# Zero rows, first loads and chunk loads of a kernel that joins delta-rule attention, a routed expert layer and a gated layer

## The chip, the cores and the metric

One core of a Trainium2 chip runs the whole program. The metric is the time of one execution on the device in microseconds (us); the median of three runs is quoted. The engines are TensorE (PE, matmuls; PEld its weight loads), VectorE (DVE), ScalarE (ACT), GpSimd (POOL) and SyncE (SP), which only issues transfers here.

## The reference, cut to what matters

Attention (4 batches, 8 heads, 768 steps, 48 wide) is a recurrence over a 48 x 48 state:

```
for t in range(S):
    y[t]  = q[t] @ state
    state = state + beta[t] * outer(k[t], v[t] - k[t] @ state)      # k normalised
```

Its 3072 x 384 output goes through eight experts, each token through the one with the largest gate logit:

```
h  = relu(x[mask] @ w1[e]);  ye = h @ w2[e]                # 384 -> 1024 -> 384
out[mask] = gate_w[mask] * sigmoid(x @ w_output_gate)[mask, e] * ye
```

and the result through `(sigmoid(x @ w_gate) * (x @ w_val)) @ w_out` with 1536 hidden columns.

## The kernel before

**Attention** runs over `NCH` = 12 chunks of 64 steps, all heads and batches at once. For a chunk c: PE adds what the old state gives to the negated values (`KU`), ACT copies that to `W`, PE applies the upper half of the inverse of a triangular matrix (`XT`, `XW`), ACT copies the result to `UF`, PE couples the two 32-step halves (`GS`), and `W`, `XT` and `UF` come once more; then PE updates the state sum (`Sps`), ACT copies it to `SH`, and PE makes the chunk's output rows (`GY`), which ACT copies to `XG`. So a chunk is one chain that goes to and fro between PE and ACT. Beside it run: the Gram products of chunk c + `LA` = c + 5 on PE (`GY<-KQ`), copied to `G`, `GS` and `PM`; on DVE the inverse for each pair of chunks, about 31 column steps of two instructions (`X<-X,tmp`, `tmp<-X,Lt`), one part of it on POOL (`tmpG`); the masks `PM`; the scaling of the values `VT`; and the gates of the expert layer. All engines' orders in attention are fixed at build time by a list with due times (`Filler`); a helper on line 78 records each operation, so most rows bear L78.

**Loads in attention** are issued by SP, in the program's order: for each chunk K and Q (`KQ`, four transfers of 192 KB into a ring of `RK` = 7 buffers), `VT` and `kt` (eight transfers of 48 KB each, two buffers each). `load_kq(c + 6)` stands in the first half of chunk c, `load_v(c + 2)` and `load_k(c + 2)` at its end. The state's products read all 128 partitions of a `KQ` buffer, so the 16 partitions without data must be zero: POOL clears buffers 2 to 6 at the start, and `load_pad` loads zeros into buffers 0 and 1.

**Rows for the experts** go to `disp` in DRAM: expert e has a region of 3584 rows, and each token is scattered (by POOL) to the next free row of its expert. An expert is then read as one window of fixed length (up to 512 rows), so the rows behind its last token must hold zeros. `zero_fill` writes 512 rows of zeros (772 KB) at the start of each of the eight regions, before any token is scattered: two at the end of chunks 0, 1 and 2, two at the start of chunk 3.

**Experts** (`Experts.run`) run over nine jobs: expert 0 in two parts of 256 and 208 rows, then seven experts in the order of their counts with windows of 460 to 380 rows. `rows` loads a job's window from `disp` to `XR`; `load` loads a quarter of an expert's weights (`w1r`, `w2r`, 384 KB each, two buffers each), which ACT and DVE or POOL split in a high and a low part. SP issues these, and takes the expert's number and the row from `tab` by a register load. The last stage (L1333, L1362) is matmuls without a gap worth naming.

Of the kernel before, what the change touches and what calls it, by code (L numbers as in the profile page):

```python
# [22 lines left out]
NE, DF = 8, 1024  # L23
# [108 lines left out]
class Attention:  # L132
# [5 lines left out]
    def run(self, small, acc, zero_fill, small_loads):  # L138
# [39 lines left out]
        quads = [(2 * a + k, 2 * y + r) for a in range(4) for r in range(2) for k, y in ((0, 0), (1, 1), (0, 1), (1, 0))]  # L178
        pairs = [(4 * z + j, z ^ y) for j in range(4) for z in range(2) for y in range(2)]

        def load_kq(c, k=slice(0, 2)):
            for r in range(2):
                d = slice(64 * r, 64 * r + 48)
                for i in range(2):
                    SP.dma_start(
                        out=KQ[c % RK][d, k].rearrange("d k p (i t) h -> d k p i (t h)", i=2)[:, :, :, i],
                        in_=a["st"][2 * c + i, d].rearrange("d (k p x) -> d k p x", k=2, p=2)[:, k])

# [11 lines left out]
                for i in range(2):  # L200
                    SP.dma_start(out=t[quad(at(b), i), par(b)], in_=a[name][32 * b : 32 * b + 32, 2 * c + i])

        def load_k(c):
            KTOK[c] = wk.tile([128, 2, 384], F32, tag="kt", name="kt", bufs=2)
            load_tok(KTOK[c], "ktok", c, pos)

        def load_v(c):
            VT[c] = wk.tile([128, 2, 384], F32, tag="VT", name="VT", bufs=2)
            load_tok(VT[c], "vtok", c, pos)

        def k_turn(c):
# [336 lines left out]
                f()  # L548

        busy(two("KU")[:, 0], W0)  # L550
        for i in range(2, RK):
            G.memset(KQ[i].rearrange("p k y t h -> p (k y t h)"), 0.0)
        for e in range(2):
            load_kq(e, slice(0, 1))
        for x in range(2):
            for i in range(2):
                for r in range(2):
                    for c2 in range(2):
                        d, o = 64 * x + 32 * i + 16 * c2 + 8 * r, 32 * (2 * x + r) + 8 * (2 * c2 + i)
                        SP.dma_start(out=be[d : d + 8], in_=a["beta"][o : o + 8])  # L560
        for t in SHT:
            V.memset(t.rearrange("p y h e -> p (y h e)"), 0.0)
        SHz = SHT[0].rearrange("p y h e -> p y (h e)")
# [1 line left out]
        zrow = ep.tile([128, 2 * ROW], F32, name="zrow")  # L565
        G.memset(zrow, 0.0)
        small_loads(V, SP)
        for e in range(2):
            load_kq(e, slice(1, 2))
        load_kq(2)  # L570
        load_v(0)
        load_kq(3)
        load_kq(4)
        load_k(0)
        load_kq(5)
# [59 lines left out]
            A.copy(out=W, in_=KU[:, :, 0:384])  # L635
            return W.rearrange("p k (a r e) -> p k a r e", a=4, r=2)

        load_pad(1)
        KU = kv(0)
        Wv = w_evac(KU)  # L640
        k_turn(0)
# [12 lines left out]
        for c in range(NCH):  # L654
# [3 lines left out]
            if c == NCH - 2:  # L658
                early.close()

            for e in (6, 7) if c == 3 else ():
                zero_fill(SP, e, zrow)
            beside(c, "load", engines)
            S0 = SH
            if c > 0:
# [21 lines left out]
                Yp = two("GY")  # L687
                y_mm(pairs[:8])
            beside(c, "KS", engines)
            if c > 0 and c + RK - 1 < NCH:  # L690
                load_kq(c + RK - 1)
            for h, b in sorted(quads, key=lambda x: x[0] % 2) if c == 0 else quads:
                mm(out=at(KUv, quad(pos(b), 0), h, b), lhsT=xt(c, h, b, 0), rhs=at(Wv, quad(cross(h, b), 0), h, b), start=True, stop=True)
            if c == 0:
# [4 lines left out]
            A.copy(out=UF, in_=KU[:, :, 0:384])  # L699
            if more:  # L700
                gp_evac(c + LA, 0, P)
            if not last:
                vm = fil.add([(0.9, 0.0, lambda c=c: v_mul(c + 1, (0, 1), V))])
            if c > 0:
# [27 lines left out]
            beside(c, "U", engines)  # L732
            if more:
                gp_evac(c + LA, 1, P)
            if c > 0:
                gate_l(2 * c - 2, mm)
                if c % 2 == 1 and 1 < c < NCH - 3:
                    gate_r(g - 1, mm)
                gate_t(2 * c - 1)
# [15 lines left out]
            if more or c == 0:  # L755
                Yp = two("GY")
                if c > 0:
                    y_mm()
                    A.copy(out=seen, in_=Yp[:, :, 383:384])
            if c > 0:  # L760
                gate_l(2 * c - 1, mm)
# [12 lines left out]
            if last:  # L774
# [5 lines left out]
                scatter(2 * c - 2)  # L780
                scatter(2 * c - 1)
                break
            if c == 1:
                load_pad(0)
            if c + 2 < NCH:
                load_v(c + 2)
                load_k(c + 2)
            if c == 0:
                zero2, other2, ops2 = inv_ops(2, SHE[2])
                fil.add(sum(prep(2), []) + [later(ops2)], WP0)  # L790
                zero2()
            elif (c + LA) % 2 == 1 and (c + LA) // 2 < NG:
                e = (c + LA) // 2
                zero, other, inv = inv_ops(e, SHE[e])
                zero()
                fil.add(sum(prep(e), []) + [later(inv)], WP)
            for e in range(2 * c, min(2 * c + 2, 6)):
                zero_fill(SP, e, zrow)
            beside(c, "end", engines)
            beside(c, "W", engines) if not last else None  # L800
            if more:
# [88 lines left out]
class Experts:  # L890


    def __init__(self, tc, a, disp, perm, idt, sp, jobs):
        self.tc, self.a, self.disp, self.perm, self.idt, self.sp, self.jobs = tc, a, disp, perm, idt, sp, jobs
        self.ahead = min(2, len(jobs))
        nc = tc.nc
        self.use((nc.vector, nc.scalar, nc.gpsimd, nc.tensor, nc.sync))
        self.blocks = [(k, j) for k in range(len(jobs)) for j in range(4) if not jobs[k].shares]
        self.raw, self.W, self.XR, self.X = {}, {}, {}, {}
        self.n_raw = self.n_split = self.nw = 0  # L900
        self.keep = {}

    def use(self, engines):
        self.V, self.A, self.G, self.T, self.SP = engines

    def rows(self, k):
        job = self.jobs[k]
        XR = self.sp.tile([XMAX // 4, 4, ROW], F32, tag="XR", name="XR", bufs=self.ahead)[0 : job.read // 4]
        self.SP.dma_start(out=XR.rearrange("p r c -> p (r c)"), in_=self.disp[ds(job.row, job.read)].rearrange("(p r) c -> p (r c)", r=4))
        self.XR[k] = XR  # L910
        self.X[k] = [self.sp.tile([128, 3, WMAX], F32R, tag=t, name=t, bufs=self.ahead)[:, :, 0 : job.n] for t in ("xh", "xl")]

    def x_scale(self, k, engines):
        n = self.jobs[k].n // 4
# [23 lines left out]
        for c in range(3):  # L938
            self.x_turn(k, c)

    def load(self, upto):

        sp = self.sp
        while self.n_raw < min(upto, len(self.blocks)):
            k, j = self.blocks[self.n_raw]
            r1 = sp.tile([128, 3, 256], F32, tag="w1r", name="w1r", bufs=2)
            r2 = sp.tile([128, 2, 384], F32, tag="w2r", name="w2r", bufs=2)
            one = lambda w: w[ds(self.jobs[k].e, 1)].rearrange("o a b -> (o a) b")
            self.SP.dma_start(out=r1, in_=one(self.a["w1"])[:, 256 * j : 256 * j + 256].rearrange("(c p) f -> p c f", p=128))
            self.SP.dma_start(out=r2, in_=one(self.a["w2"])[256 * j : 256 * j + 256].rearrange("(k p) d -> p k d", p=128))  # L950
            self.raw[self.n_raw] = r1, r2
            self.n_raw += 1
# [95 lines left out]
def kernel_body(tc, a, out):  # L1048
    nc = tc.nc
    V, A, G, T, SP = nc.vector, nc.scalar, nc.gpsimd, nc.tensor, nc.sync  # L1050
    with ExitStack() as ctx:
# [11 lines left out]
        if True:  # L1063
# [17 lines left out]
            def beside(c, at, engines, ps=None):  # L1081

                V, A, G, T, SP = engines
                at = c - NCH, at
                if at == (-2, "load"):
                    sp = moe.enter_context(tc.tile_pool(name="ex_s", bufs=1, side="left", reuse_waits="tile"))
                    ex.append(Experts(tc, a, disp, perm, small["idt"], sp, jobs))
                    ex[0].use(engines)
                    ex[0].load(2)
                elif at == (-2, "U"):  # L1090
                    ex[0].high(0)
                elif at == (-2, "W"):
                    ex[0].low(0, 0, V)
                    ex[0].low(0, 1, V)
                elif at == (-2, "rows"):
                    ex[0].load(3)
                    ex[0].rows(0)
                elif at == (-2, "end"):
                    ex[0].high(1)
                elif at == (-1, "KS"):  # L1100
                    ex[0].x_scale(0, (V,))
                elif at == (-1, "U"):
                    ex[0].low(1, 0, V)
                    ex[0].low(1, 1, V)
                elif at == (-1, "rows"):
                    ex[0].load(4)
                elif at == (-1, "W"):
                    ex[0].x_turn(0, 0, ps)
                elif at == (-1, "V"):
                    ex[0].x_turn(0, 1, ps)  # L1110
                elif at == (-1, "Y"):
                    ex[0].x_turn(0, 2, ps)
# [10 lines left out]
            oh = yp.tile([1, 7, 7], F32, name="oh")  # L1123
            cw = yp.tile([1, 2, 24], F32, name="cw")
            tab = yp.tile([1, 18], I32, name="tab")
            wins, nums, names = [cst[0:1, 296 + 7 * i : 303 + 7 * i] for i in range(3)]

            def order():
# [17 lines left out]
                V.tensor_tensor(out=c[:, 1:2], in0=cnt[:, 0:1], in1=c[:, 0:1], op=ALU.subtract)  # L1146
                V.tensor_scalar_min(out=c[:, 1:2], in0=c[:, 1:2], scalar1=float(E1))
                V.reduce_sum(out=c[:, 2:9], in_=gt, axis=AXX)
                V.tensor_tensor(out=c[:, 2:9], in0=c[:, 2:9], in1=wins, op=ALU.min)
                for i, d in enumerate((1, 2, 4, 8)):  # L1150
                    V.tensor_tensor(out=cw[:, 1 - i % 2, 8:17], in0=cw[:, i % 2, 8:17], in1=cw[:, i % 2, 8 - d : 17 - d], op=ALU.add)
# [4 lines left out]
                    jobs[r + 2].e, jobs[r + 2].row = e, e * STRIDE  # L1156
                for k in range(1, 9):
                    jobs[k].off = nc.values_load(tab[0:1, 7 + k : 8 + k], engines=engs, min_val=0, max_val=NTOK, skip_runtime_bounds_check_because=why)

            def gv_src(i):  # L1160
                b, w = divmod(i, 2)
# [14 lines left out]
            def hook(q, f):  # L1176
# [14 lines left out]
                elif i == 3:  # L1191
                    order()
                    E.rows(1)
                    E.load(6)
                if i == QX:
                    E.x_scale(1, (E.V, E.A))
# [252 lines left out]
```

## Time and profile before

| | |
|---|---|
| median of 3 runs | 985.54 us (985.51 to 987.24) |
| profiled execution: its own time, its span | 988.84 us, 987.1 us |
| PE, DVE, ACT, POOL busy | 932.0, 498.7, 363.5, 386.1 us |
| granted PE clock, mean | 0.933 of full |
| attention | from the start to about 280 us |
| experts, beginning with the end of attention | about 280 to 526 us |
| gated layer | 526 to 977 us |

Busy time says little about PE, since its matmuls overlap. What counts is the time in which an engine waits: a row gives it in brackets with what ended it. The program is one chain of stages, so time that one stage loses, or gains, moves all that follows.

### The profile page before, as it was taken

What the parts mean: (1) busy time and instruction counts of PE and PEld (TensorE: products, weight loads), DVE (VectorE), ACT (ScalarE), POOL (GpSimd) and SP (SyncE); (2) the same over time, 40 slices, a digit from 0 to 9 for tenths busy, and PEclk for the clock granted to TensorE, in tenths of its full rate; (3) what the DMA queues carried; (4) which work ended last, traced back from release to release, by engine and by line L of the source; (5) the groups of instructions that cost most, each with busy time, mean ns of one, the idle gap of its engine ahead of it and who ended that gap; (6) DMA issues with size and microseconds to landing.
All of it is one profiled execution on the core that took longest, in us unless ns stands there. A gap on an engine that the chain in (4) does not pass through costs nothing. (4 is left out here: it accounts for less than half of the span.)

```text
span 987.1 us, 23362 instructions
## 1 busy us (share of the span) xinstructions
PE 932.0 (94%) x9557; PEld 820.6 (83%) x9558; DVE 498.7 (51%) x1387; ACT 363.5 (37%) x670; POOL 386.1 (39%) x550
## 2 busy tenths in 40 slices
PE   6777899988899999999999999999999999999997
PEld 5666687776789899999998888888888888888886
DVE  7999978994354577777865554113113112011112
ACT  2553464554634455555552222112112112111111
POOL 7362364652132455776651434223222212322122
PEclk8697798795879999999999999999999999999999
DMA  5878755224225556466522220000000000000000
GB/s 123 156 168 177 205 119 119 66 71 127 75 90 192 158 167 188 151 202 189 167 66 50 80 64 25 9 1 17 17 1 16 16 1 9 25 1 9 25 1 32
DMA packets 63057, 83.31 MB, mean 84 GB/s; under 512 B 10377, under 2 KB 55698, under 8 KB 62946
## 3 DMA queue, kind: packets, MB, share of 16 engines
q1 hardware_dynamic: 59234, 71.01, 27.2%
q0 software_dynamic: 3712, 10.78, 3.2%
q8 instruction: 75, 1.23, 0.5%
q14 instruction: 36, 0.29, 0.1%
HBM read 64.65 MB, written 15.80 MB: 81 GB/s over the span
## 5 line engine op out<-in xcount | busy, mean ns | idle before, releaser
L1370 DVE TENSOR_TENSOR gf<-gf,g 128x512 f32<-128x512 f32 x72 | 49.4, 686 | 304.9 <-PE g L1362 304.2
L840 POOL TENSOR_TENSOR gsl<-gf,gsh 128x512 fp32r<-128x512 f32 x65 | 84.7, 1304 | 269.7 <-ACT gsh L839 269.7
L1369 ACT ACTIVATE gf<-g 128x512 f32<-128x512 f32 x72 | 43.0, 597 | 181.8 <-PE g L1362 180.4
L839 ACT CAST gsh<-gf 128x512 fp32r<-128x512 f32 x69 | 42.8, 621 | 147.7 <-DVE gf L1370 147.6
L1333 PE MATMUL o<-wol,gsh 128*128 128x384 f32 x272 | 87.1, 339 | 0.0
L1333 PE MATMUL o<-woh,gsl 128*128 128x384 f32 x272 | 86.6, 336 | 0.0
L78 DVE TENSOR_TENSOR X<-X,tmp 128x84 f32<-128x84 f32 (+31 forms) x303 | 72.2, 267 | 0.9
L78 DVE TENSOR_TENSOR tmp<-X,Lt 128x84 f32<-128x84 f32 (+31 forms) x303 | 71.7, 266 | 1.5
L1333 PE MATMUL o<-woh,gsh 128*128 128x384 f32 x272 | 63.3, 340 | 0.0
L969 POOL TENSOR_TENSOR w1l<-w1r,w1h 128x256 fp32r<-128x256 f32 x57 | 52.6, 949 | 25.5 <-ACT w1h L961 21.9
L1362 PE MATMUL g<-yl,wgh 128*128 128x512 f32 x216 | 62.5, 394 | 0.0
L1362 PE MATMUL g<-yl,wvh 128*128 128x512 f32 x216 | 62.4, 395 | 0.0
L1362 PE MATMUL g<-yh,wgh 128*128 128x512 f32 x180 | 60.3, 394 | 0.0
L993 PE MATMUL y<-hh,w2h 128*128 128x460 f32 (+6 forms) x168 | 60.0, 357 | 0.0
L993 PE MATMUL y<-hh,w2l 128*128 128x460 f32 (+6 forms) x168 | 58.5, 348 | 0.0
L1035 DVE SCALAR_TENSOR_TENSOR hl<-h,hh 128x460 fp32r<-128x460 f32 (+7 forms) x57 | 33.0, 579 | 50.0 <-ACT hh L1034 49.9
L78 PE MATMUL GY<-KQ 48*64 48x128 f32 (+1 forms) x640 | 44.3, 405 | 14.5 <-DMA KQ<-in_st_dram 10.8
L1333 PEld LDWEIGHTS o<-woh,gsh 128*128 128x128 f32 x272 | 49.7, 188 | 6.7 <-ACT woh L839 0.6
L1333 PEld LDWEIGHTS o<-wol,gsh 128*128 128x128 f32 x272 | 50.5, 188 | 2.3
L1362 PE MATMUL g<-yh,wgl 128*128 128x512 f32 x180 | 51.8, 394 | 0.0
L1362 PE MATMUL g<-yh,wvl 128*128 128x512 f32 x180 | 51.6, 394 | 0.0
L1362 PE MATMUL g<-yh,wvh 128*128 128x512 f32 x180 | 51.6, 394 | 0.0
(327 smaller groups left out, 2199.0 us busy)
## 6 DMA issues: line engine op xcount, KB each, us to landing
w1r<-in_w_dram SPq DMA_DIRECT2D x32, 384.0 KB
w2r<-in_w_dram SPq DMA_DIRECT2D x32, 384.0 KB
KQ<-in_st_dram SPq DMA_DIRECT2D x40, 192.0 KB
disp<-zrow SPq DMA_DIRECT2D x8, 772.0 KB
VT<-in_vtok_dram SPq DMA_DIRECT2D x96, 48.0 KB
kt<-in_ktok_dram SPq DMA_DIRECT2D x96, 48.0 KB
XG<-in_m2g_dram SPq DMA_DIRECT2D x12, 384.0 KB
XG<-in_m2v_dram SPq DMA_DIRECT2D x12, 384.0 KB
```

What stands on the lines that cost most here:

```text
L78: r = f(*args, **kw)
L839: (act or nc.scalar).copy(out=hi, in_=src)
L840: eng.tensor_tensor(out=lo, in0=src, in1=hi, op=ALU.subtract)
L969: engine.tensor_tensor(out=l[:, k], in0=r[:, k], in1=h[:, k], op=ALU.subtract)
L993: m = self.T.matmul(out=ys[c][:, 0:n], lhsT=w2[l][:, f % 2, 128 * c : 128 * c + 128], rhs=(hh, hl)[r], start=(f == 0 and i == 0), stop=(f ...
L1035: self.behind = self.V.scalar_tensor_tensor(out=hl, in0=hp[:, 0:n], scalar=0.0, in1=hh, op0=ALU.max, op1=ALU.subtract).ins
L1333: T.matmul(out=ops_[m][:, 0:384], lhsT=gh[l][:, 128 * m : 128 * m + 128], rhs=wo[r][:, f], start=(f == 0 and i == 0), stop=(f == 11 and i ...
L1362: T.matmul(out=ps, lhsT=gv[w][l][:, c, 128 * f : 128 * f + 128], rhs=Y[r][c], start=(i == 0 and c == 0), stop=(i == 2 and c == 2))
L1369: A.activation(out=gf, in_=gps[0], func=AF.Sigmoid)
L1370: V.tensor_tensor(out=gf, in0=gf, in1=gps[1], op=ALU.mult)
```

## The change

The rows behind an expert's last token are cleared later and from another source: only expert 0's region is still filled in attention (`zero_fill(SP, 0, zrow)`); for each of the other seven, `clear(k)` copies zeros, once the counts are known, from the padding of the input `st` in DRAM to `disp` from the end of the expert's tokens on, as many rows as the window has. The row where they end comes from a new table `ends` through a register load on SP. `clear(2)` stands behind the load of job 1's rows, each later one behind the load of the job before.

The first loads are split over engines: of the first halves (K) of chunks 0 and 1, SP issues two transfers and ACT two for each; of the 16 transfers of beta ACT issues 4, POOL 4 and SP 8. DVE clears buffer 1 of `KQ`, which did without before, and `load_pad(1)` is gone. The whole loads of `KQ` 2 and 3 move ahead of the second halves (Q) of chunks 0 and 1.

A chunk's loads come in four parts: K of chunk c + 7 behind the state's products of chunk c, `VT` of c + 2 behind the first `UF`, `kt` behind the second, Q of c + 7 behind the products with the state. ACT writes one element of the `VT` or `kt` buffer first (`hold`), and the transfers into that buffer wait for this write. The second quarter of the first expert's weights gets such a hold, too.

```
-        def load_kq(c, k=slice(0, 2)):
+        def load_kq(c, k=slice(0, 2), engines=(SP, SP)):
...
-                    SP.dma_start(
+                    engines[r].dma_start(
...
+        def hold(t):
+
+            A.copy(out=t[0:1, 0, 0:1], in_=idt[0:1, 0:1])
+
-        def load_k(c):
+        def load_k(c, wait=False):
             KTOK[c] = wk.tile([128, 2, 384], F32, tag="kt", name="kt", bufs=2)
+            if wait:
+                hold(KTOK[c])
             load_tok(KTOK[c], "ktok", c, pos)
...
-        for i in range(2, RK):
-            G.memset(KQ[i].rearrange("p k y t h -> p (k y t h)"), 0.0)
+        clear = lambda E, i: E.memset(KQ[i].rearrange("p k y t h -> p (k y t h)"), 0.0)
+        clear(V, 1)
         for e in range(2):
-            load_kq(e, slice(0, 1))
+            load_kq(e, slice(0, 1), (SP, A))
...
-                        SP.dma_start(out=be[d : d + 8], in_=a["beta"][o : o + 8])
+                        (A, G, SP, SP)[n % 4].dma_start(out=be[d : d + 8], in_=a["beta"][o : o + 8])
+                        n += 1
+        for i in range(2, RK):
+            clear(G, i)
+        load_kq(2)
...
+        load_kq(3)
         for e in range(2):
             load_kq(e, slice(1, 2))
-        load_kq(2)
         load_v(0)
-        load_kq(3)
...
-        load_pad(1)
...
-            for e in (6, 7) if c == 3 else ():
-                zero_fill(SP, e, zrow)
...
-            if c > 0 and c + RK - 1 < NCH:
-                load_kq(c + RK - 1)
+            if c > 0 and c + RK < NCH:
+                load_kq(c + RK, slice(0, 1))
...
+            if c > 0 and c + 2 < NCH:
+                load_v(c + 2, True)
...
+            if c > 0 and c + 2 < NCH:
+                load_k(c + 2, True)
...
+                    if c + RK < NCH:
+                        load_kq(c + RK, slice(1, 2))
...
-            if c == 1:
+            if c == 0:
+                load_v(2)
+                load_k(2)
                 load_pad(0)
-            if c + 2 < NCH:
-                load_v(c + 2)
-                load_k(c + 2)
-            if c == 0:
+                load_kq(RK)
...
-            for e in range(2 * c, min(2 * c + 2, 6)):
-                zero_fill(SP, e, zrow)
+            if c == 0:
+                zero_fill(SP, 0, zrow)
...
+        if 1 < k < len(self.jobs) - 1:
+            self.clear(k + 1)
...
-                    ex[0].load(2)
+                    ex[0].load(1)
+                elif at == (-2, "KS"):
+                    ex[0].load(2, A)
...
+                V.scalar_tensor_tensor(out=ends[:, 0:7], in0=key[:, 0:7], scalar=float(STRIDE), in1=c[:, 2:9], op0=ALU.mult, op1=ALU.add)
...
+            def clear(k):
+
+                n = jobs[k].read
+                end = nc.values_load(ends[0:1, k - 2 : k - 1], engines=[ET.SP], min_val=STRIDE, max_val=NE * STRIDE - XMAX, skip_runtime_bounds_check_because="made from counts of distinct tokens")
+                E.SP.dma_start(out=disp[ds(end, n)].rearrange("(s q r) c -> s q (r c)", q=16, r=2), in_=a["st"][0 : n // 32, 48:64, 0 : 2 * ROW])
```

The order of PE's instructions stays as it was; DVE gets two instructions more (the clear of the buffer and `ends`), ACT 19 holds. Three places show what moves.

SP at the start of the program before, from its first transfer on (KQ_95 to KQ_99 are the ring's buffers 0 to 4, be is beta, disp the experts' rows):

```order
L80 DMA KQ_95<-in_st_dram 48x2x256
L78 DMA KQ_95<-in_st_dram 48x2x256 x3
L78 DMA KQ_96<-in_st_dram 48x2x256 x4
L78 DMA be<-in_beta_dram 8x192 x16
L78 DMA cst<-in_cst_dram 128x320
L78 DMA wgo<-in_wgo_dram 128x48
L78 DMA KQ_95<-in_st_dram 48x2x256 x4
L78 DMA KQ_96<-in_st_dram 48x2x256 x4
L78 DMA KQ_97<-in_st_dram 48x4x256 x4
L78 DMA VT<-in_vtok_dram 32x384 x8
L78 DMA KQ_98<-in_st_dram 48x4x256 x4
```

And the same place of the change:

```order
L80 DMA KQ_95<-in_st_dram 48x2x256
L78 DMA KQ_95<-in_st_dram 48x2x256
L78 DMA KQ_96<-in_st_dram 48x2x256 x2
L78 DMA be<-in_beta_dram 8x192 x8
L78 DMA KQ_97<-in_st_dram 48x4x256 x4
L78 DMA cst<-in_cst_dram 128x320
L78 DMA wgo<-in_wgo_dram 128x48
L78 DMA KQ_98<-in_st_dram 48x4x256 x4
L78 DMA KQ_95<-in_st_dram 48x2x256 x4
L78 DMA KQ_96<-in_st_dram 48x2x256 x4
L78 DMA VT<-in_vtok_dram 32x384 x8
```

Twelve transfers have left SP, buffers 2 and 3 come before the Q halves of 0 and 1, and `VT` of chunk 0 comes behind 30 of SP's transfers where it was behind 38, with one whole buffer (number 3) more ahead of it.

SP in attention before, from the first fill to the last four, that is behind chunk 0 to the start of chunk 3:

```order
L78 DMA disp<-zrow 256x1x772 x2
L78 DMA KQ_95<-in_st_dram 48x4x256 x4
L78 DMA KQ_95<-in_st_dram 16x2x1024 x2
L78 DMA VT<-in_vtok_dram 32x384 x8
L78 DMA kt<-in_ktok_dram 32x384 x8
L78 DMA disp<-zrow 256x1x772 x2
L78 DMA KQ_96<-in_st_dram 48x4x256 x4
L78 DMA VT<-in_vtok_dram 32x384 x8
L78 DMA kt<-in_ktok_dram 32x384 x8
L78 DMA disp<-zrow 256x1x772 x4
```

And of the change, from the one fill left through chunks 1 and 2:

```order
L78 DMA disp<-zrow 256x1x772
L78 DMA KQ_96<-in_st_dram 48x2x256 x4
L78 DMA VT<-in_vtok_dram 32x384 x8
L78 DMA kt<-in_ktok_dram 32x384 x8
L78 DMA KQ_96<-in_st_dram 48x2x256 x4
L78 DMA KQ_97<-in_st_dram 48x2x256 x4
L78 DMA VT<-in_vtok_dram 32x384 x8
L78 DMA kt<-in_ktok_dram 32x384 x8
```

Seven fills are gone, and K and Q of a chunk stand on both sides of its `VT` and `kt`.

SP at the start of the experts before, from the load of job 1's rows (the second XR of 64 partitions) to the load of job 2's rows:

```order
L78 DMA XR<-disp 64x1544
L1155 TENSOR_LOAD tab
L78 ISA
L78 DMA w1r<-in_w_dram 128x3x256
L78 ISA
L78 DMA w2r<-in_w_dram 128x2x384
L78 ISA
L78 DMA w1r<-in_w_dram 128x3x256
L78 ISA
L78 DMA w2r<-in_w_dram 128x2x384
L78 DMA perm<-XR 1x256
```

And of the change:

```order
L78 DMA XR<-disp 64x1544
L1186 TENSOR_LOAD ends
L78 ISA
L78 DMA disp<-in_st_dram 256x1x772
L1178 TENSOR_LOAD tab
L78 ISA
L78 DMA w1r<-in_w_dram 128x3x256
L78 ISA
L78 DMA w2r<-in_w_dram 128x2x384
L78 ISA
L78 DMA w1r<-in_w_dram 128x3x256
```

A register load and the clear of 512 rows stand ahead of the next four loads of weights. In the later jobs the clear (448 or 384 rows) stands one or two loads of weights behind the `XR` that it follows.

## Rows read from the trace of the kernel before

**Rows 1.** The page: span, the instruction queue, the fill's issues

```profile
span 987.1 us, 23362 instructions
...
q8 instruction: 75, 1.23, 0.5%
...
disp<-zrow SPq DMA_DIRECT2D x8, 772.0 KB
```

**Rows 2.** Windows: busy us of each engine, PE clock, DMA share, GB/s

```profile
100.00:120.00 20.00, 15.68 (x395) 12.66 (x395) 19.06 (x83) 8.80 (x17) 8.56 (x16) 0.76 0.85 236
160.00:180.00 20.00, 18.75 (x499) 15.60 (x498) 19.70 (x82) 11.85 (x24) 11.80 (x23) 0.83 0.28 70
350.00:400.00 50.00, 50.00 (x272) 46.84 (x271) 34.22 (x56) 27.17 (x49) 30.57 (x42) 1.00 0.60 176
```

**Rows 3.** Timeline, PEld: start, duration, what, idle before and its end

```profile
5.14 0.19 PEld L78 LDWEIGHTS XTP<-KQ 48*64 48x64 f32 x1 [0.20 <-issue]
...
95.09 0.52 PEld L78 LDWEIGHTS GY<-KQ 48*64 48x64 f32 x9 [2.29 <-issue]
...
119.81 0.12 PEld L78 LDWEIGHTS KU<-W,XT 32*32 32x32 f32 x1 [2.39 <-issue]
```

**Rows 4.** Timeline, PE, chunks 1 and 2

```profile
61.01 2.84 PE L78 MATMUL KU<-SH,KQ 128*64 128x96 f32 x32 [3.21 <-DMA KQ<-in_st_dram]
...
82.04 1.30 PE L78 MATMUL GY<-UF,PM 64*64 64x48 f32 x36 [3.43 <-issue]
...
88.75 0.23 PE L78 MATMUL KU<-W,XW 32*32 32x48 f32 x1 [0.18 <-DVE XW L78]
```

**Rows 5.** Timeline, DVE: two of its waits in attention

```profile
44.39 1.99 DVE L78 STREAM_TRANSPOSE Lt<-G 128x1024 f32<-128x1024 f32 x1 [1.29 <-DMA G<-GS]
...
128.15 0.19 DVE L78 TENSOR_TENSOR g_m<-GL,cst 128x32 f32<-128x32 f32 x1 [5.49 <-PE GL L78]
```

**Rows 6.** Timeline, ACT: the first W of chunks 2, 4, 5, 6, 8, 9, 10

```profile
86.16 0.80 ACT L78 COPY W<-KU 128x768 f32<-128x768 f32 x1 [1.33 <-PE KU L78]
...
131.44 0.80 ACT L78 COPY W<-KU 128x768 f32<-128x768 f32 x1 [0.26 <-issue]
...
148.57 0.80 ACT L78 COPY W<-KU 128x768 f32<-128x768 f32 x1 [0.25 <-PE KU L78]
...
168.32 0.80 ACT L78 COPY W<-KU 128x768 f32<-128x768 f32 x1 [0.26 <-PE KU L78]
...
204.74 0.80 ACT L78 COPY W<-KU 128x768 f32<-128x768 f32 x1 [0.18 <-PE KU L78]
...
219.88 0.80 ACT L78 COPY W<-KU 128x768 f32<-128x768 f32 x1 [0.90 <-PE KU L78]
...
243.94 0.80 ACT L78 COPY W<-KU 128x768 f32<-128x768 f32 x1 [1.31 <-PE KU L78]
```

**Rows 7.** Timeline, SP's issues: beta, KQ 3 and 4, fills, weights

```profile
4.71 6.74 SPq L78 DMA_DIRECT2D be<-in_beta_dram  x16
...
24.30 6.25 SPq L78 DMA_DIRECT2D KQ<-in_st_dram  x8
...
104.72 4.11 SPq L78 DMA_DIRECT2D disp<-zrow  x4
...
226.53 0.49 SPq L78 DMA_DIRECT2D w2r<-in_w_dram  x1
```

**Rows 8.** Timeline, ACT: a small copy and the next instruction

```profile
57.46 0.16 ACT L78 COPY seen<-KU 128x2 f32<-128x2 f32 x1
57.52 1.58 ACT L78 COPY KH<-kt 128x768 f32<-128x768 f32 x1
```

**Rows 9.** Timeline, SP and ACT at the start of the experts

```profile
294.87 0.41 SPq L78 DMA_DIRECT2D w1r<-in_w_dram  x1
...
297.22 1.13 ACT L78 ACTIVATE XR<-XR 52x384 f32<-52x384 f32 x2 [0.86 <-DMA XR<-disp]
...
306.48 0.83 ACT L78 CAST w1h<-w1r 128x768 fp32r<-128x768 f32 x1
```

More of the change, by code (lines that the diff above doesn't have):

```diff
@@ L201, in load_tok, with load_v @@
                     SP.dma_start(out=t[quad(at(b), i), par(b)], in_=a[name][32 * b : 32 * b + 32, 2 * c + i])
-        def load_k(c):
+        def hold(t):
+            A.copy(out=t[0:1, 0, 0:1], in_=idt[0:1, 0:1])
+        def load_k(c, wait=False):
             KTOK[c] = wk.tile([128, 2, 384], F32, tag="kt", name="kt", bufs=2)
+            if wait:
+                hold(KTOK[c])
             load_tok(KTOK[c], "ktok", c, pos)
-        def load_v(c):
+        def load_v(c, wait=False):
             VT[c] = wk.tile([128, 2, 384], F32, tag="VT", name="VT", bufs=2)
+            if wait:
+                hold(VT[c])
             load_tok(VT[c], "vtok", c, pos)
@@ L550, in run @@
         busy(two("KU")[:, 0], W0)
-        for i in range(2, RK):
-            G.memset(KQ[i].rearrange("p k y t h -> p (k y t h)"), 0.0)
+        clear = lambda E, i: E.memset(KQ[i].rearrange("p k y t h -> p (k y t h)"), 0.0)
+        clear(V, 1)
         for e in range(2):
-            load_kq(e, slice(0, 1))
+            load_kq(e, slice(0, 1), (SP, A))
+        n = 0
         for x in range(2):
@@ L901, in __init__ @@
         self.keep = {}
+        self.clear = lambda k: None
     def use(self, engines):
@@ L939, in x_prep, with load @@
             self.x_turn(k, c)
-    def load(self, upto):
+    def load(self, upto, behind=None):
         sp = self.sp
@@ L947, in load @@
             r2 = sp.tile([128, 2, 384], F32, tag="w2r", name="w2r", bufs=2)
+            if behind is not None:
+                behind.copy(out=r1[0:1, 0, 0:1], in_=self.idt[0:1, 0:1])
             one = lambda w: w[ds(self.jobs[k].e, 1)].rearrange("o a b -> (o a) b")
@@ L1125, in kernel_body @@
             tab = yp.tile([1, 18], I32, name="tab")
+            ends = yp.tile([1, 8], I32, name="ends")
             wins, nums, names = [cst[0:1, 296 + 7 * i : 303 + 7 * i] for i in range(3)]
@@ L1193, in hook @@
                     E.rows(1)
+                    E.clear = clear
+                    clear(2)
                     E.load(6)
```

## The prediction

> **What bounds the kernel now.** I read the page first: PE is busy for most of the span, and the span is 987.1 us [rows 1]. The share hides three stages, so I went to the windows of 20 us. From 350 to 400 us, among the experts, PE is busy for 50.00 of 50.00 us at the full clock, with DMA at 0.60 of its time; from 100 to 120 us, in attention, it is busy for 15.68 of 20, its granted clock is 0.76, and DMA is busy 0.85 at 236 GB/s [rows 2]. So time is to be had in attention, and there the question is which engine is late.
>
> DVE is busy for 19.06 of 20 us there [rows 2] and looks like the bound. Its waits say otherwise from chunk 2 on: at 128.15 it waits 5.49 us for PE [rows 5]. PE in turn waited for DVE at 88.75, for the inverse of chunks 2 and 3, for 0.18 us only [rows 4]. The reader is to see the order: up to 88.75 DVE is the slower by a hair, and what PE loses before it is absorbed; behind it PE is late, and DVE loses 5.49 us to it.
>
> What makes PE late? Its rows name no engine: a run of like weight loads breaks off for 2.29 us at 95.09, another for 2.39 us at 119.81, with "issue" as the reason, which means that nothing the profile knows was waited for [rows 3]. The page has a queue of 75 packets and 1.23 MB named instruction, 16 KB each [rows 1]: the program itself comes by DMA. Four fills are issued from 104.72 on, over 4.11 us [rows 7]; their 3.1 MB at 236 GB/s [rows 2] last 13 us, until about 118, and the second break ends at 119.81. I take the breaks for instructions that come late behind the fills.
>
> A rule speaks against that. The Trainium skill (Runtime: NRT & Kernel Launch, section Instruction fetch mechanics) has a stream of instructions fetched ahead in blocks of 16 KiB over a DMA queue of the sequencer, with the cost of a block mostly hidden. The size agrees with the 1.23 MB in 75 packets [rows 1]; that it is hidden doesn't agree with the breaks of 2.29 and 2.39 us [rows 3], if they are fetches. By the rule the fills cost PE nothing, and the second term below, 8.4 us, would be nought; that is among the rivals.
>
> **Chunks 2 and 3, the main term.** The first `W` of a chunk marks its start [rows 6]. Chunks 2 and 3 take 131.44 - 86.16 = 45.28 us. Chunk 4 takes 17.13 and chunk 5 takes 19.75, with the same work, `VT` and `kt` loading, and no fill. The change takes seven of eight fills, 772 KB each [rows 1], out of these chunks; the mean of 4 and 5, twice, is 36.88. Gain 8.4 us; bounds: twice chunk 4, 11.0, twice chunk 5, 5.8. It hangs on DVE keeping up. DVE has 5.49 us of waiting for PE to give back [rows 5], and 1.29 from the next term; PE would come 8.4 + 1.3 earlier, so some 3 us must come from the slack between what DVE delivers and what PE takes. No wait of PE in attention behind 88.75 names DVE, so there is slack, but its size no row tells.
>
> **The start.** K of chunk 1 may land earlier, but PE goes from its warm-up into the products of chunk 0 at 5.14 with 0.20 us idle, and that for nothing the profile shows [rows 3]: earlier data gains nothing, nought on both sides unless ACT's transfers come late. DVE's clear of buffer 1 stands ahead of two of SP's and two of ACT's loads; the clears of `SHT` behind it have time until DVE's first copies. The 16 transfers of beta took SP 6.74 us, and it reached `KQ` 3 and 4 at 24.30 [rows 7]; now 12 transfers fewer and `KQ` 3 ahead of the Q halves. Chunk 3's Gram matrix so comes sooner, and DVE's wait of 1.29 us for it at 44.39 [rows 5] can go: gain 1.3, bounds 0 and 1.3. PE's waits of 3.21 us for a `KQ` at 61.01 (the pad of buffer 1, which is gone) and of 3.43 at 82.04 [rows 4] lie ahead of 88.75: PE will arrive there early and wait for DVE instead. I count nothing for them.
>
> **Chunk 9.** It takes 243.94 - 219.88 = 24.06 us, chunk 8 before it 15.14 [rows 6]: 8.9 us more. Four loads of weights, 1.5 MB, have been issued by 226.53 [rows 7], in its middle. Now two come behind `kt` of chunk 11, whose hold stands late in chunk 9, and two behind a hold in chunk 10. The bytes stay, and chunk 9 has gates that chunk 8 hasn't; I take 2 us, bounds 0 and 5.
>
> **Holds.** 19 copies of one element on ACT. A copy of two elements lasts 0.16 us, but the next instruction starts 0.06 us later [rows 8]. Behind each stand the copies of `XTP` and `W` or `SH`. Price: 0.06 to 0.16 us each where ACT is the late one, nought where it waits for PE; so from 0 to 19 x 0.16 = 3.0 in all. I take 1.0: twelve stand in chunks 1 to 6, where ACT copies Gram products as well, at 0.08 each.
>
> **Clears among the experts.** Each reads and writes up to 772 KB in DRAM. No row shows such a transfer; at the 236 GB/s of the fills' window [rows 2] one lasts 3.3 us. The bound below is nought (PE is always busy and the weights come ahead); above, each of seven stops PE for its length: 23 us. I take 0.5, all of it at the first: it can't start before job 1's rows have landed, at 297.22 when ACT gets them [rows 9], and the weights that SP issued at 294.87 then come behind it, some 3.5 us later in issue and 3.3 in transfer. They are wanted at 306.48 [rows 9], 11.6 us after the old issue: 4.8 us are left for a load of 384 KB, 1.7 us at the same rate, and for the three behind it the slack is thin. Later clears stand between loads that wait for their buffers anyway; what is queued behind them is the second half of a block's weights, wanted a block later.
>
> **Sum.** -8.4 - 1.3 - 2 + 1.0 + 0.5 = -10.2 us. The profiled execution took 988.84 us for its span of 987.1, so its like would take 978.6; the runs shown lie 3.3 lower, at 985.54, which gives 975.3. I say 975.5.
>
> **Rivals.** Differences under 0.2% (2 us, 983.6 to 987.5) are about what a measurement here can't tell from no change.
>
> *The spread loads break PE's stream as the fills did.* Chunks 2 and 3 only come down to chunk 5's 19.75, chunk 9 stays: -5.8 - 1.3 + 1.5 = -5.6, 979.9. For it: chunk 5 is 2.6 us longer than chunk 4 without a fill [rows 6]. Against: PE's clock is 0.83 at a DMA share of 0.28 [rows 2], with no long break.
>
> *All of it goes.* Chunks 2 and 3 like chunk 4, chunk 9 gains 5: -11.0 - 1.3 - 5 = -17.3, 968.2. For it: a PE with fewer gaps may be granted more clock than 0.76 [rows 2].
>
> *The breaks aren't the fills' work, or DVE sets the pace anyway.* Then only 1.3 is gained and the holds cost 1: 985.2, no change. For it: DVE at 19.06 of 20 [rows 2]. Against: its 5.49 us of waiting [rows 5], and a break where the fills end. The rule of the Trainium skill named above would have this case.
>
> *Slower: clears hold SP.* SP is one queue in order; a clear waits for the rows ahead of it to land and the weights wait behind it. If each of seven costs PE more than 1.5 us, the gain is gone; at 3.3 us each it is 23: 985.5 - 10.2 + 23 = 998. Against: the full PE windows with weights loaded a block ahead [rows 2].
>
> **How the numbers follow.** Forecast 0.56, spread loads 0.16, all of it 0.10, no change 0.09, slower 0.09. The forecast's own bounds: 5.8 + 0 + 0 - 3 - 3 at worst, of which I don't believe all together, and 17.3 at best. The range takes in the forecast, the spread loads and all but the edge of "all of it", and reaches up to the edge of no change: 967.5 to 984. Faster 0.82, same 0.09, slower 0.09.
>
> **What would show it.** Right: chunks 2 and 3 near 37 us from `W` to `W`, no wait of PE over 2 us with "issue" in them, DVE's 5.49 gone, its wait at 44 gone, chunk 9 near 22, the experts' length unchanged from the first full window on. Wrong: DVE's `XW` waited for by PE in chunk 4 or 6 for microseconds (DVE was the bound); breaks of the same length in a window with a DMA share of 0.3 (not the fills); ACT or PE waiting for weights or `XR` at the start of the experts (the clears).

## The result, and the profile after

The changed kernel takes 977.38 us, the median of four runs (976.99 to 980.66), and the kernel before, run beside it, 986.19 us (985.51 to 987.24). The ratio is 0.9917, with a 95% interval from 0.9893 to 0.9941: faster by 8.8 us, where 10.2 were forecast. The forecast of 975.5 us was 1.9 us low, and its range held the time. That the sum came out is not the same as that each term did: of its five terms only the main one did.

First the same windows as [rows 2], in the kernel after (columns as there):

```profile
100.00:120.00 20.00, 18.21 (x523) 15.15 (x517) 19.54 (x88) 12.59 (x27) 7.42 (x18) 1.00 0.42 107
160.00:180.00 20.00, 19.34 (x498) 15.99 (x498) 18.50 (x85) 10.86 (x22) 14.73 (x32) 0.74 0.28 75
350.00:400.00 50.00, 48.77 (x267) 46.09 (x266) 33.46 (x57) 25.95 (x48) 31.14 (x42) 1.00 0.69 212
```

From 100 to 120 us DMA is busy for 0.42 of its time instead of 0.85, PE for 18.21 us instead of 15.68, and PE's granted clock is full instead of 0.76. Among the experts the bytes of the fills have come back as clears (DMA 0.69 instead of 0.60).

The waits of PE's weight loads from chunk 2's inverse to chunk 4, in the kernel before (89 to 131 us) and after (89.5 to 131 us); the columns are the sum in us, how many, and the longest:

```profile
PEld GY L78 <- issue: 4.5, 3, 2.3
PEld KU L78 <- issue: 4.4, 5, 2.4
...
PEld Sps L78 <- issue: 0.9, 1, 0.9
```

```profile
PEld KU L78 <- issue: 1.5, 4, 0.4
PEld Sps L78 <- issue: 1.3, 1, 1.3
PEld GY L78 <- issue: 1.3, 3, 0.6
```

The breaks that no engine answers for have shrunk from 9.8 us to 4.1, and the two above 2 us [rows 3] are gone, as is DVE's wait of 5.49 us for PE [rows 5]. So far all is as forecast. The first `W` of chunks 2, 4, 8, 9 and 10 in the timeline of ACT, from the same view as [rows 6], says more:

```profile
81.41 0.80 ACT L78 COPY W<-KU 128x768 f32<-128x768 f32 x1 [0.23 <-PE KU L78]
...
124.28 0.80 ACT L78 COPY W<-KU 128x768 f32<-128x768 f32 x1 [0.24 <-PE KU L78]
...
198.57 0.80 ACT L78 COPY W<-KU 128x768 f32<-128x768 f32 x1 [0.59 <-PE KU L78]
...
216.76 0.80 ACT L78 COPY W<-KU 128x768 f32<-128x768 f32 x1 [0.65 <-PE KU L78]
...
238.71 0.80 ACT L78 COPY W<-KU 128x768 f32<-128x768 f32 x1 [0.87 <-PE KU L78]
```

Chunks 2 and 3 take 124.28 - 81.41 = 42.87 us and not the 37 foretold. PE's timeline in chunk 2 (first), and DVE's at two of its transpositions (second), tell why:

```profile
89.25 0.34 PE L78 MATMUL KU<-W,XT 32*32 32x48 f32 x2 [5.75 <-DVE XT L78]
```

```profile
45.71 2.04 DVE L78 STREAM_TRANSPOSE Lt<-G 128x1024 f32<-128x1024 f32 x1 [2.09 <-DMA G<-GS]
...
87.09 2.01 DVE L78 STREAM_TRANSPOSE XT<-X 128x1024 f32<-128x1024 f32 x1
```

PE is early at chunk 2, as foretold, and waits there for DVE's inverse. But DVE itself is late: its `Lt` comes at 45.71 instead of 44.39 [rows 5], and its wait for the Gram matrix, which was to go, has grown from 1.29 to 2.09 us. The `XT` that PE waits for came at 85.58 before. So the fair measure of the main term is not from `W` to `W` but from DVE's `XT` of chunks 2 and 3 to chunk 4's `W`: 131.44 - 85.58 = 45.86 before, 124.28 - 87.09 = 37.19 after. Cutting both traces at five rows gives the whole account (us; the second pair of traces is from another chip, experiments e5 and e6 below):

| stretch | before | after | difference | second pair |
|---|---|---|---|---|
| start to DVE's `XT` of chunks 2 and 3 | 85.58 | 87.09 | +1.5 | 84.60 to 87.19: +2.6 |
| to `W` of chunk 4 | 45.86 | 37.19 | -8.7 | 46.31 to 36.53: -9.8 |
| to `W` of chunk 11 | 126.99 | 129.11 | +2.1 | 116.58 to 117.68: +1.1 |
| to ACT's first `XR` of job 1 | 38.79 | 36.90 | -1.9 | 36.85 to 35.01: -1.8 |
| to the end | 689.88 | 688.71 | -1.2 | 690.46 to 688.09: -2.4 |
| sum | 987.1 | 979.0 | -8.1 | -10.3 |

### The profile page after: what moved, and what is told of

It reads as the page before. It is cut to its first block, busy times and chain, and to the rows that moved or that the text cites. A ratio compares the mean times of both kernels' runs of the same rounds, so it can differ in the third digit from the quotient of the medians.

```text
span 979.0 us, 23428 instructions
## 1 busy us (share of the span) xinstructions
PE 925.2 (95%) x9557; PEld 816.2 (83%) x9558; DVE 501.0 (51%) x1389; ACT 364.9 (37%) x689; POOL 387.2 (40%) x554
## 4 chain that ended last, share of the span: by engine, by line
PE 82%; DVE 7%; DMA 3%; ACT 3%; issue 2%; POOL 2%; SPq 0%; POOLq 0%; DVEq 0%; ACTq 0%
PE g L1393 29%; PE o L1364 14%; PE h L1050 10%; PE y L1012 9%; PE KU L78 6%; PE GY L78 5%; PE h L78 2%; PE y L78 2%; PE Sps L78 1%; PE GL L78 1%; DVE tmp L78 1%; DVE X L78 1%; PE XTP L78 1%; ACT UF L78 1%; DMA XR<-disp 1%
```

## The experiments

The fills are the cause by my theory. The rivals: DVE or the start decides; the spread loads do it; the fills hurt by their place and not by their traffic. e1 to e4 shared a chip, e5 to e8 another, e9 to e12 a third; the kernel before took 977.05, 977.11 and 976.44 us there, so ratios are compared across them. The table has the results; the last three columns come from each profile: the start of DVE's `XT` of chunks 2 and 3, from there to chunk 4's `W`, and from there to the `XT` of chunks 10 and 11.

| run | median us | ratio and interval | `XT` 2 | to `W` 4 | to `XT` 10 |
|---|---|---|---|---|---|
| e1 fills only | 967.20 | 0.9904 [0.9873, 0.9934] | 84.27 | 39.20 | 137.46 |
| e2 fills back | 973.23 | 0.9955 [0.9933, 0.9977] | 86.42 | 42.48 | 137.68 |
| e3 fills and clears | 970.31 | 0.9927 [0.9901, 0.9953] | 86.98 | 43.23 | 137.97 |
| e4 Q first | 967.35 | 0.9921 [0.9888, 0.9953] | 84.75 | 36.85 | 135.34 |
| e5 before again | 976.45 | one run | 84.60 | 46.31 | 143.94 |
| e6 after again | 966.27 | 0.9900 [0.9867, 0.9933] | 87.19 | 36.53 | 135.27 |
| e7 old start | 965.76 | 0.9891 [0.9859, 0.9922] | 84.18 | 36.26 | 135.40 |
| e8 loads whole | 966.42 | 0.9899 [0.9866, 0.9932] | 87.40 | 37.66 | 137.07 |
| e9 late fills | 970.67 | 0.9940 [0.9917, 0.9963] | 86.72 | 35.87 | 136.92 |
| e10 paced fills | 968.15 | 0.9908 [0.9875, 0.9940] | 87.78 | 37.37 | 135.53 |
| e11 old start, no holds | 966.51 | 0.9898 [0.9870, 0.9926] | 84.41 | 36.39 | 135.69 |
| e12 weights together | 969.35 | 0.9922 [0.9891, 0.9953] | 86.69 | 36.59 | 135.35 |

**e1, the fills alone.** The kernel before, with this and the clears:

```
-            for e in (6, 7) if c == 3 else ():
-                zero_fill(SP, e, zrow)
...
-            for e in range(2 * c, min(2 * c + 2, 6)):
-                zero_fill(SP, e, zrow)
+            if c == 0:
+                zero_fill(SP, 0, zrow)
```

> The kernel before with one part of the change: seven of the eight fills taken out of attention and the clears put among the experts; first loads and chunk loads stay as they were. If the fills' traffic breaks PE's stream (the prediction's step): chunks 2 and 3 take some 37 us from W to W instead of 45.28, no break over 2 us between 88 and 132, and the time is 986.2 - 8.4 + 0.5 = 978. If the breaks are not the fills' work, or DVE sets the pace: chunks 2 and 3 keep their 45 us and the time is 986. If the spread of a chunk's loads is needed as well, it lies between, near 982.

0.9904, as much as the whole change gives in e6. From `XT` to `W` 39.20 us, 7 less than in e5, and no break above 1.2 us but the wait for `XT`; from `W` to `W` it is 123.47 - 83.27 = 40.20 where some 37 were expected. The main step holds by itself; that it needs the spread loads falls.

**e2 and e3, the fills back.** The change with the two pieces above restored, without the clears (e2) and with them (e3).

> The change without its clears, the eight fills back at their old places in attention; first loads and chunk loads as changed. If the fills cost what the prediction has for them: 977.4 + 8.4 - 0.5 = 985.3, with the breaks of PE back in chunks 2 and 3. If they cost only together with the old chunk loads: under 980.

> The change with its clears, and the eight fills in attention as well (rows are cleared twice). The difference to the run with the fills alone is the price of the seven clears: 0.5 us by the prediction, up to 23 by the rival in which they hold SP; the experts' length says the same without the runs' scatter.

The fills cost 6.0 and 6.7 us from `XT` to `W` against e6, and in all 0.9955 and 0.9927 against 0.9900, some 5 and 3 us: less than the 8.4 expected. The stretches from `XT` to `W` as windows (columns as in [rows 2]), e5, e2, e3 and e6 in this order:

```profile
84.60:130.91 46.31, 40.52 (x985) 32.73 (x983) 39.01 (x164) 21.95 (x42) 16.40 (x37) 0.70 0.75 193
...
86.42:128.90 42.48, 38.55 (x949) 31.48 (x951) 39.58 (x164) 21.27 (x46) 14.20 (x37) 0.68 0.62 191
...
86.98:130.21 43.23, 37.93 (x949) 31.04 (x951) 39.60 (x164) 21.24 (x45) 14.13 (x37) 0.69 0.63 191
...
87.19:123.72 36.53, 32.77 (x949) 27.49 (x950) 35.60 (x141) 21.21 (x45) 12.92 (x35) 0.87 0.36 90
```

The last three hold the same 949 matmuls. Of the 5.95 us that e2 takes more than e6, 5.78 are busy time of PE and 0.17 idle time; in e3 5.16 of 6.70 are busy time. The breaks that were expected did not come back at their old length: behind the wait for `XT`, e2's longest idle time of PE's weight loads is 1.2 us, and e3 has one of 1.97. What came back with the fills is a lower granted clock: 0.68 and 0.69 here, 0.70 and 0.71 in the two traces of the kernel before, but 0.78 to 0.91 in the other ten traces, which have no whole fill in this stretch. So most of the price goes with the clock, and not with the breaks. Shorter windows of e3 (first fence) and of e6 (second) show both:

```profile
110.00:115.00 5.00, 4.40 (x171) 3.58 (x167) 4.88 (x20) 3.17 (x9) 0.00 (x0) 0.91 1.02 390
115.00:120.00 5.00, 3.22 (x92) 2.54 (x84) 4.97 (x28) 0.57 (x1) 0.00 (x0) 0.50 1.04 293
120.00:125.00 5.00, 5.00 (x92) 3.39 (x92) 4.15 (x12) 3.43 (x9) 1.03 (x2) 0.57 0.44 107
```

```profile
115.00:120.00 5.00, 4.19 (x108) 3.33 (x105) 4.85 (x28) 2.99 (x8) 1.02 (x2) 1.00 0.38 91
120.00:125.00 5.00, 5.00 (x134) 4.75 (x134) 4.90 (x18) 3.94 (x6) 0.00 (x0) 1.00 0.47 119
```

While four fills run (390 GB/s), PE's granted clock falls to 0.50, the lower level of 1.2 GHz, where e6 has 1.00; PE's one long stop, 1.78 us up to 118.02, comes after the fall. What that level costs is read from one group of 64 equal matmuls in chunk 2, at 0.50 in e2 (first) and behind the rise to full clock in e6 (second):

```profile
98.60 1.53 PE L78 MATMUL Sps<-UF,KH 64*48 64x48 f32 x64
```

```profile
98.24 0.94 PE L78 MATMUL Sps<-UF,KH 64*48 64x48 f32 x64
```

The clears can be priced here: from ACT's first `XR` of job 1 to the end e2 takes 970.5 - 281.60 = 688.9 us and e3, with seven clears, 970.3 - 281.80 = 688.5. They cost nothing that shows.

**e4, Q first.** The change, but:

```
-        load_kq(2)
...
-        load_kq(3)
         for e in range(2):
             load_kq(e, slice(1, 2))
+        load_kq(2)
         load_v(0)
+        load_kq(3)
```

> The change with the second halves (Q) of chunks 0 and 1 ahead of the whole loads of buffers 2 and 3 again, as in the kernel before; first K and beta still by three engines. My reading of the trace of the change: PE waits 11.7 us for Q, and DVE's second pair of transposes comes at 45.71 instead of 44.39, which DVE, never idle after 62, carries on to chunk 2 (XT at 87.09 instead of 85.58). If so, DVE's transposes come at 44.4 or sooner and 1.3 us are gained: 976.1. If DVE's lateness there is absorbed later: 977.4, no change.

The mechanism was right: DVE's timeline has

```profile
43.42 1.98 DVE L78 STREAM_TRANSPOSE Lt<-G 128x1024 f32<-128x1024 f32 x1
```

with no wait, and `XT` at 84.75. But the time doesn't tell: 0.9921 where the change has 0.9900, well within the intervals. In its profiled run PE waited 2.4 us for an activation just behind the experts, which no other profile shows, and gave back there what it had won.

**e5 to e8, the parts beside the whole.** e5 and e6 are the two kernels unchanged.

> The kernel before, unchanged, for a profile beside the next three: chunks 2 and 3 near 45 us with two breaks over 2 us of PE, whatever the granted clock; no theory differs on it.

> The whole change, unchanged, as the yardstick for the parts: a ratio of 0.992 as at first. If the fills are the whole of it, its ratio is that of the fills alone (0.990), and its first loads and its spread loads together bring nothing.

e7 has the first loads of the kernel before: SP alone, in the old order, with the zeros for buffer 1.

```
-            load_kq(e, slice(0, 1), (SP, A))
+            load_kq(e, slice(0, 1))
...
-                        (A, G, SP, SP)[n % 4].dma_start(out=be[d : d + 8], in_=a["beta"][o : o + 8])
+                        SP.dma_start(out=be[d : d + 8], in_=a["beta"][o : o + 8])
...
+        load_pad(1)
```

> The change with all first loads as in the kernel before (SP alone, K of 0 and 1, beta, Q, then buffers 2 and 3; zeros loaded into buffer 1's padding); fills, clears and chunk loads as changed. If the changed start costs DVE 1.3 us (second transposes at 45.71 instead of 44.39), this is 1.3 us or more faster than the change, with the transposes at 44.4 or sooner. If PE's earlier finish of chunks 0 and 1 (without the zeros for buffer 1 to wait for) counts as well, it is no faster. The prediction had the changed start gain 1.3, so by it this run is 1.3 slower.

e8 has a chunk's loads whole and at their old places.

```
-            if c > 0 and c + RK < NCH:
-                load_kq(c + RK, slice(0, 1))
+            if c > 0 and c + RK - 1 < NCH:
+                load_kq(c + RK - 1)
...
-                load_v(c + 2, True)
...
-                load_k(c + 2, True)
```

> The change with a chunk's loads whole and at their old places (K and Q of chunk c + 6 in the first half of chunk c, VT and kt of c + 2 at its end, no holds); fills, clears and start as changed. If spreading gains nothing and the holds cost 1.0 us, as predicted: 1 us faster than the change. If the whole loads crowd PE's stream as the fills did: some us slower, in chunks 4 to 8.

e7's `XT` is 3.0 us earlier than e6's and its profiled span 2.4 us shorter (962.1 against 964.5); its median is 0.5 us lower, which the intervals can't tell from nothing. e8 can't be told from e6 either. So the changed start loses 2 to 3 us of DVE's time, and the spreading gains 1.1 us from `XT` to `W` (37.66 to 36.53; with the old start, from e1 to e7, 2.9), of which the time shows nothing.

**e9 and e10, the same traffic elsewhere.** e9 is the change with seven more fills into rows that nobody reads, two at the end of chunks 4, 5 and 6, one at the start of chunk 7; e10 has them in eight parts each, spread over chunks 1 to 7.

```
+            SP.dma_start(out=junk[512 * i : 512 * i + 512].rearrange("(p a r) c -> p a (r c)", a=2, r=2), in_=zrow.unsqueeze(1).to_broadcast([128, 2, 2 * ROW]))
```

> The whole change, and seven fills more of 772 KB each, of the same source and shape as the old ones, into rows of DRAM that nobody reads: two at the end of chunks 4, 5 and 6, one at the start of chunk 7, where DVE does not set the pace as it does up to chunk 2. If the fills' traffic is what breaks PE's stream, and lets the granted clock fall behind the break: chunks 4 to 7 together grow by some 5 to 8 us, with breaks of 2 us and a clock of 0.5 in stretches that follow them, and the time goes up by as much, ratio 0.996 to 0.998. If what hurt was the fills' place (the loads of the first chunks behind them, or DVE's pace): no more than 2 us, ratio 0.992.

> The whole change, and the same seven fills into rows that nobody reads, but each in eight parts of 96 KB that are spread over one chunk, chunks 1 to 7. If it is the burst (the DMA engines busy all of their time for microseconds) that breaks PE's stream: no cost, ratio 0.990 to 0.992. If it is the bytes: some 5 to 8 us as with whole fills, ratio 0.996 to 0.998. SP issues 56 transfers more; if that holds up the loads, PE or DVE waits for KQ, VT or kt.

SP came to issue the last three of e9 in a row, at 174.38. PE's timeline in e9 (first) and the same group in e6 (second):

```profile
179.84 0.97 PE L78 MATMUL GY<-SH,KQ 128*64 128x96 f32 x10
183.95 0.65 PE L78 MATMUL GY<-SH,KQ 128*64 128x96 f32 x6 [3.14 <-issue]
```

```profile
181.79 1.57 PE L78 MATMUL GY<-SH,KQ 128*64 128x96 f32 x16
```

A run of 16 equal products stops after ten, for 3.14 us. All that the other six read was there for the first ten. What wasn't there shows in the queues of e9 from 172.4 to 181.2 us (first), in e9 from 181.2 to 181.8 (second) and in e6 from 172.4 to 181.2 (third); columns: packets, MB, share of the DMA engines:

```profile
q1 hardware_dynamic: 922, 2.33, 73.4%
q14 instruction: 1, 0.01, 0.4%
```

```profile
q1 hardware_dynamic: 77, 0.21, 97.7%
q8 instruction: 1, 0.02, 10.0%
```

```profile
q1 hardware_dynamic: 301, 0.30, 14.5%
q8 instruction: 2, 0.03, 1.5%
```

In 8.8 us of the burst no packet of the instruction queue q8 started, where e6 had two; one started in the next 0.6 us and took 0.96 us (10.0% of 16 engines in 0.6 us), and PE went on at 183.95. The rule of the Trainium skill (Runtime: NRT & Kernel Launch, Instruction fetch mechanics), that blocks are fetched ahead and the cost is mostly hidden, agrees with e6 in this stretch and doesn't agree with the burst of e9. The packets of all fourteen traces bear the reading out: between 60 and 260 us PE stops 32 times for 0.7 us or more inside a group of like matmuls with no engine named, and each time it goes on 1.2 to 1.8 us after a q8 packet has ended. Not all of these stops need fills: e1 has one of 1.53 us at 146.05, with whole chunk loads and a DMA share of 1.08 and 0.94 around it, and e6 one of 1.25 us at 187.33. The six above 1.6 us are three in the two traces of the kernel before and one each in e9, e10 and e12. Then the clock, in windows of e9:

```profile
175.00:180.00 5.00, 4.56 (x171) 4.08 (x169) 4.76 (x25) 3.06 (x7) 3.89 (x12) 1.00 0.91 344
180.00:185.00 5.00, 1.86 (x40) 1.56 (x44) 3.44 (x17) 1.02 (x3) 4.43 (x7) 0.94 0.89 273
185.00:190.00 5.00, 5.00 (x144) 4.00 (x136) 4.65 (x16) 2.00 (x4) 0.02 (x1) 0.50 0.38 99
```

Full up to the break, 0.50 behind it. The order isn't always this one. In the kernel before the clock was down while PE was still busy, and the break [rows 3] followed:

```profile
92.00:93.00 1.00, 1.00 (x23) 0.77 (x15) 1.00 (x6) 0.58 (x1) 0.84 (x3) 0.50 0.98 261
93.00:94.00 1.00, 0.23 (x3) 0.00 (x0) 0.96 (x5) 0.00 (x0) 0.80 (x3) 0.50 1.16 190
```

So the long break can't be what lowered the clock there; how the fills do it no run singles out. e9 costs 0.0040 against e6, 3.9 us, and 4.2 us against e11 on the same chip, so fills cost time in chunks 4 to 7 too: the place alone isn't it. But it costs less than 5 to 8: of seven fills two pairs passed with breaks of 1.0 us at most, and only the three in a row stopped PE for longer. (A pair can do it too: the break at 95.09 in the kernel before has two fills ahead of it, issued at 86.40, with whole chunk loads right behind them.) In e10 the waits of PE's weight loads between 90.5 and 190 us are

```profile
PEld KU L78 <- issue: 4.6, 13, 0.7
PEld KU L78 <- ACT UF L78: 4.2, 5, 1.2
PEld GY L78 <- issue: 3.7, 4, 1.2
```

none above 1.2 us, with the same bytes, and its ratio of 0.9908 is within the change's own interval. Its interval overlaps that of e9, too, so by the time alone the two can't be told apart.

**e11 and e12, holds and weights.** e11 is e7 without the holds (`load_v(c + 2)` and `load_k(c + 2)` in their new places, without `True`); e12 is the change with

```
-                    ex[0].load(1)
-                elif at == (-2, "KS"):
-                    ex[0].load(2, A)
+                    ex[0].load(2)
```

> The change with the first loads of the kernel before, and without the holds of VT and kt (their transfers wait for the buffer's readers alone): the parts that the earlier runs speak for. If the holds cost the predicted 1.0 us, or part of it: 0.5 to 1 us under the run with the old start, ratio 0.988 to 0.989. If they cost nothing or their transfers now come too early: the same, 0.989 to 0.991.

> The change with the first expert's first two quarters of weights loaded together again, without the hold. If moving the second pair out of chunk 9 was worth the predicted 2 us: chunk 9 is 2 us longer than in the change's run beside it (16.5 to 18.7) and the time 2 us higher. If the stall of chunk 9 only goes into chunk 8: chunks 8 and 9 together stay at 33 to 34 us and the time stays.

e11 with 0.9898 against 0.9891 for e7: the holds cost nothing that can be measured. In e12 chunk 9 takes 16.9 us and 16.5 in e6, so it doesn't grow, but chunk 10 does, 18.3 us against 14.9. SP issues four loads, 1.5 MB, in a row from 222.14 on there, and PE's weight loads stop in the same manner as behind three fills (e12 first; then e10, whose weights are loaded as in the change):

```profile
233.07 0.91 PEld L78 LDWEIGHTS GY<-SH,KQ 128*64 128x64 f32 x12 [2.61 <-issue]
...
234.08 0.98 PEld L78 LDWEIGHTS GY<-SH,KQ 128*64 128x64 f32 x12 [3.09 <-issue]
```

In e10 the four loads came as close together in spite of the hold, from 225.04 to 228.88, and its chunk 10 took 19.1 us. So such a stop follows four loads in a row, but e12 doesn't show that loading them together is what brings it on.

e12's ratio is 0.0022 above e6's, inside the intervals.

No run beats the change by more than its interval; e7 has the lowest ratio.

## Why the prediction was right, point by point

*Chunks 2 and 3, -8.4.* Right in size and, in the main, in cause: -8.7, and -9.8 on the second chip, from `XT` to `W`; e1 has 7.1 of the 9.8 with the fills alone, e2 and e3 give 6.0 to 6.7 back, and the rest is that of the spread loads and the start. The foretold "37 us from `W` to `W`" was the wrong measure, since PE's earlier arrival at chunk 2, which the prediction itself spoke of, becomes a wait there. But "I take the breaks for instructions that come late behind the fills" is the smaller part of it. On the second chip PE's idle time from `XT` to `W` fell by 2.0 us (5.79 to 3.76) and its busy time by 7.8 (40.52 to 32.77), at a granted clock of 0.70 and then 0.87; on the first chip the same windows give 2.8 and 5.9, at 0.71 and 0.86. The term took the clock in without a name, by pricing whole chunks, so that the size came out owes something to luck.

*The start, -1.3.* Wrong in sign: +1.5 and +2.6. The failed step is "Chunk 3's Gram matrix so comes sooner". SP's order was read, PE's was not: PE's order is fixed, and the masked products of chunks 0 and 1, which read the Q halves, stand ahead of chunk 2's and 3's Gram matrices. Q now comes behind two more whole buffers, and the timelines of PE and ACT after have

```profile
22.70 0.47 PE L78 MATMUL GY<-KQ 48*64 48x64 f32 x2 [11.71 <-DMA KQ<-in_st_dram]
```

```profile
26.04 1.02 ACT L78 COPY PM<-GY 128x1024 f32<-128x1024 f32 x1 [13.77 <-PE GY L78]
```

e4 and e7 put it right with the old order (`XT` at 84.75 and 84.18); with K and beta by three engines in e4 and by SP alone in e7, they lie 0.6 us apart. That an earlier K gains nothing was right.

*Chunk 9, -2.* Chunk 9 came out as said (24.06 to 238.71 - 216.76 = 21.95; 18.6 to 16.5 on the second chip), but chunk 8 grew by 3.0 (15.14 to 216.76 - 198.57 = 18.19; 13.3 to 17.2). The term is nought or a loss. In e6 PE waits 2.2 us in chunk 8 for DVE's scaled values; in the first trace no such wait, but a clock of 0.72 there. That both have one cause was not shown. Nor is it the split of the weights that shortened chunk 9: in e12, with them together, it takes 16.9 us.

*Holds, +1.0,* and *clears, +0.5.* Both nought within what was measured (e11, e3). The first clear did push the weights behind it on SP, as reckoned, and nothing waited:

```profile
285.99 0.50 SPq L78 DMA_DIRECT2D XR<-disp  x1
287.86 0.67 SPq L78 DMA_DIRECT2D disp<-in_st_dram  x1
289.15 0.43 SPq L78 DMA_DIRECT2D w1r<-in_w_dram  x1
```

*The slack.* The prediction needed "some 3 us" from DVE's slack and could not tell its size. The last column of the experiments' table does: DVE needs 135.3 to 135.7 us for four pairs of chunks in the six kernels with spread loads, different starts and no whole fill but the first (e4, e6, e7, e10, e11, e12), 137.1 and 137.5 with whole loads (e8, e1), and 143.94 in e5. DVE's waits in e6 between 62 and 222 us are, all of them,

```profile
DVE VT L78 <- DMA VT<-in_vtok_dram: 0.3, 2, 0.2
DVE VT L78 <- issue: 0.2, 1, 0.2
```

so that DVE is the bound of attention there: that is where the rest of a faster PE goes. It doesn't explain why the times of e4, e7 and e11 aren't below that of e6: in them DVE's `XT` of chunks 2 and 3 is 2.4 to 3.0 us earlier. e7's profiled span is shorter by 2.4 us, e11's by 0.1 (964.4 against 964.5), and no median shows it; that stays open. In the first trace after it is not quite so: 140.19 us, with a clock of 0.83 between 120 and 190 us where e6 has 0.93. It also fits that the fills cost 5 us in e2 and 3 in e3, and not 8.4: PE lost 6.0 and 6.7 us to them, DVE only 2.4 and 2.7.

*The rivals.* That spread loads break PE fell (e8, no breaks after). That all of it goes fell (DVE). That the fills aren't it, with the rule of hidden fetches, fell (e1, e9). That clears hold SP fell (e3; the experts' length is 1.2 us less, not more).

*Open.* The 1.9 and 1.2 us gained behind chunk 11 (1.8 and 2.4 in the second pair) no run singles out; two traces of the kernel before are few, and from chunk 11 to job 1's `XR` the variants of the changed kernel themselves take between 33.5 us (e9) and 37.1 us (e2). Without these 3.1 us, which the prediction didn't have, the first pair of traces would differ by 5.0 us and not by 8.1: that the sum came within 1.4 us of the measured gain is partly luck.

## What to carry to other kernels

Price a bulk transfer by what it does to the engine with the densest instruction stream, not only by what waits for its data. One sign is a wait without a releaser, in the middle of equal instructions, beside DMA engines at their limit; the other, here the dearer one, is equal instructions that last longer at a lower granted clock. So compare busy time and clock, not only waits. Move such transfers to a stage with few, long instructions, or cut them into parts; here neither showed a cost. The clears among the experts come one at a time, though, so no run shows what a burst of three would do there. When loads are reordered, read the order in which the consumer's queue takes them: the first load that a fixed order wants must not move back.

## What the runs showed of the hardware that was not expected

With three fills of 772 KB in a row (344 GB/s from 175 to 180 us of e9) no 16 KB packet of instructions started on q8 for 8.8 us, where two do in e6, and PE stood for 3.14 us. In fourteen traces PE goes on from 32 stops of this kind 1.2 to 1.8 us after such a packet has ended. That PE waits for the packet is read from these times; no run moves the packets alone, and that q8 is PE's own queue is inferred: the kernel before has 75 packets on it for 19,115 matmuls and weight loads, 255 for each.

With the fills the granted clock from `XT` to `W` was 0.68 to 0.71 in four traces, and 0.78 to 0.91 in the ten without whole fills there; equal groups took 1.53 us at 0.50 and 0.94 at 1.00. In e9 the clock fell behind the break, in e3 and the kernel before ahead of it.

Among the experts a DMA share of 0.69 and 212 GB/s left PE busy for 48.77 of 50 us at the full clock (267 matmuls, where attention has 523 in 20 us), and its one wait there of over 1 us was for DVE.
